# One level of Strassen's scheme for the gate and up projections of a transformer block, in passes of 1024 tokens

## The chip, the cores and the metric

The kernel runs on one core of a Trainium2 chip. The core has five engines that each work through their own list of instructions: TensorE (PE, matrix products, with its weight loads shown apart as PEld), VectorE (DVE), ScalarE (ACT), GpSimd (POOL) and SyncE (SP), which here only issues transfers. Matmul results land in PSUM, eight banks of 512 float32 columns for each of 128 partitions; all else on the chip lives in SBUF. The metric is the device time of one execution in microseconds, given as the median over runs. Beside it stands one execution recorded by the hardware profiler, whose rows are used for all durations.

## What is computed

The reference is one block for 2048 tokens of width 1024: a modulated layer norm, linear attention with 32 heads and a gated residual, a second modulated layer norm, and a gated feed-forward network (FFN) of inner width 3584 with a gated residual.

```python
def _A_ref(x, wqkv, wo):
    ...
    pq, pk = (phi(q), phi(k))
    kv = jnp.einsum('bhsd,bhse->bhde', pk, v)
    z = jnp.einsum('bhsd->bhd', pk)
    num = jnp.einsum('bhqd,bhde->bhqe', pq, kv)
    den = jnp.einsum('bhqd,bhd->bhq', pq, z)[..., None] + 1e-06
    o = num / den
    return (lambda x, *d: x.transpose(*d))(o, 0, 2, 1, 3).reshape(B, S, D) @ wo

def _B_ref(x, w_gate, w_up, w_down):
    return _gelu(x @ w_gate) * (x @ w_up) @ w_down
x = A_x
mod = (_silu(c) @ w_mod).reshape(c.shape[0], 6, 1, -1)
sa, ca, ga, sb, cb, gb = (...)
h = _layernorm(x, axis=-1) * (1 + ca) + sa
x = x + ga * _A_ref(h, A_wqkv, A_wo)
h = _layernorm(x, axis=-1) * (1 + cb) + sb
x = x + gb * _B_ref(h, B_w_gate, B_w_up, B_w_down)
```

Inputs, weights and output are bfloat16 (bf16), sums on the chip float32. Gelu is the tanh form.

## The kernel before

The 2048 tokens are 16 chunks (`c_`) of 128, and four groups (`sg`) of four chunks. The whole of x stays in SBUF (`XALL`) and is overwritten by the block's partial results. One large byte arena holds everything, at offsets worked out by hand, and many tiles share bytes at different times.

The program is written as a list of operations on a small scheduler class, `Sched`. `op` and `dma` record, for each operation, the bytes it reads and writes, and find from these what it must wait for. Each engine then runs its own list. One stretch of the program, from `mark[0]` to `mark[1]`, is handed to `reorder` (L1441), which simulates the engines with a table of costs (`COST`) and puts the lists of DVE, ACT and POOL in order of due time. Everything else, all of TensorE's and SP's lists among it, runs in the order in which it was written. `mark[1]` is set at L1287, ahead of the first normalisation for the FFN.

The stages, with the times in the profiled execution:

- **K, Q** (to 127 us): layer norm 1, the transposed h (`H1`), keys and queries (`L811`, `L862`), and the modulation rows, which DVE adds up from `w_mod` (`mod_step`, L1005, L750).
- **M stage** (127 to 191): `m_tile` (L822, L826) builds keys transposed times x, `kv_prod` (L840, L844) and `w2_pair` (L1118) fold it with the value and output weights into one matrix `W2` of 1024 x 1024, `den` (L1143) makes the denominators, stored and loaded back as row factors (`rb_load`, L1163).
- **Attention outputs** (191 to 234.6 and four more chunks inside the FFN): `pq_scale` (L1176, L1181) scales the queries, `wo_mm` (L1184) multiplies a chunk with `W2`, 16 matmuls a chunk, and adds to x on DVE (L1197). Chunks 0 to 11 run ahead of the FFN; chunks 12 to 15 run as hooks inside the first group's FFN.
- **Layer norm 2**: `ln2_a` (L1272). For chunks 0 to 3 the sums run on ACT and POOL (`ln_stats_act`, L633), for the others on DVE while the group before is in its down projection. A DMA transposes each chunk into `H2`, and `mod2` (L714) scales it on DVE.
- **FFN**, four groups of 512 tokens. `stream_pair` (L1263) loads gate and up weights, 256 columns at a time, into one of three slots; all 7 MB of each are read again for every group. `ffn_fc` (L1318) makes one block of 128 columns: eight matmuls for gate and eight for up into two PSUM banks (L1325, L1328), then Gelu by hand: square and half on ACT, a sum-and-product on DVE, tanh on ACT, two more products on DVE (L1336 to L1343), the result in `YT`. `ffn_down` (L1345) multiplies a chunk with the down weights (56 matmuls), scales with the gate row `GBB` (L1358), adds x (L1360) and stores. The down weights (`WDT`, seven tiles of 1 MB) are loaded once, during the first group.
- The last modulation row, `GBB`, is made during the first group: `gb_load`, `gb_acc`, `gb_rows` (L1382 to L1404).

TensorE's order inside a block, and the rows of Gelu:

```python
for dc in range(NDC):
    og = sch.op(T, lambda e, dc=dc: e.matmul(PS(bg), WG[slot][:, dc, e_ * P:(e_ + 1) * P], H2[sg][:, dc, :], ...
    ou = sch.op(T, lambda e, dc=dc: e.matmul(PS(bu), WU[slot][:, dc, e_ * P:(e_ + 1) * P], H2[sg][:, dc, :], ...
```

Of the kernel before, what the change touches and what calls it, by code (L numbers as in the profile page):

```python
# [6 lines left out]
dt = mybir.dt  # L7
# [3 lines left out]
P = 128  # L11
S = 2048
D = 1024
# [10 lines left out]
NFP = NFC // 2  # L24
HP = 1040
MK = ((684, 341), (0, 342), (342, 342))

GELU_C = math.sqrt(2.0 / math.pi)
GELU_A = 0.044715
# [7 lines left out]
OFF_WD = OFF_HT + NSG * 8192  # L37
OFF_YT = OFF_WD + NFC * 2048
OFF_WS = OFF_YT + NFC * SGW * 2
# [5 lines left out]

OFF_WK = OFF_WD
OFF_WV = OFF_WD + 16384
OFF_WQ = OFF_WD + 32768
OFF_X = OFF_WD + 49152
OFF_MS3 = OFF_YT + 10 * 2048  # L50
OFF_RB = [OFF_WS + 8192, OFF_WD + 16384]
OFF_GAB = OFF_CONST
OFF_GBB = OFF_CONST + 4096
OFF_ROW = OFF_CONST + 8192
OFF_SMALL = OFF_CONST + 12288
OFF_XH2 = OFF_GAB
OFF_PK = [OFF_YT + i * 2048 for i in range(14)] + [OFF_GBB, OFF_GBB + 2048]
OFF_MB = [OFF_TMP + 8192, OFF_TMP + 10240] * 2 + [OFF_WS + i * 2048 for i in range(4)]
OFF_MTB = [OFF_TMP + 6144, OFF_GUH]
OFF_MF = [OFF_TMP + i * 1376 for i in range(2)]  # L60
OFF_MU = [OFF_TMP + i * 1376 for i in range(2, 4)]
OFF_CAR = OFF_HT + 3 * 8192
# [91 lines left out]
class Sched:  # L154
# [41 lines left out]
    def dma(self, stream, fn, rd=(), wr=(), deps=(), note="", overwrite_ok=False):  # L196
# [6 lines left out]
        if prev is not None:  # L203
# [7 lines left out]
              "modr": (0.04, 0.15), "mod": (0.028, 0.15), "w": (0.216, 0.15), "wo": (0.216, 0.15)},  # L211
        ACT_: {"exp": (0.5, 0.1), "sum": (1.19, 0.1), "sq": (1.28, 0.1), "xhata": (1.14, 0.1), "hmoda": (0.49, 0.1), "mcp": (0.38, 0.1), "zc": (0.13, 0.1),
               "mhi": (0.52, 0.1), "mrow": (0.4, 0.1), "wcp": (0.92, 0.1), "hraw": (0.92, 0.1)},
        DVE_: {"min": (0.34, 0.085), "add": (0.607, 0.085), "bn": (0.603, 0.085), "aggr": (0.124, 0.085), "ve": (0.07, 0.085), "xhat": (0.46, 0.085),
               "nm": (0.074, 0.085), "hmod": (0.25, 0.085), "macc": (0.66, 0.085), "mlo": (0.6, 0.085), "kvt": (0.21, 0.085), "z": (0.34, 0.085),
               "dene": (0.335, 0.085), "rden": (1.67, 0.085), "pqs": (0.6, 0.085), "wofold": (1.13, 0.085), "x": (1.14, 0.085)},
        POOL_: {"nmean": (0.22, 0.05), "ve": (0.22, 0.05), "rstd": (0.55, 0.05), "nm": (0.55, 0.05), "ones": (0.12, 0.05)},
        SP_: {"T": (1.25, 1.25), "Tb": (1.25, 1.25), "mT": (1.25, 1.25), "wm": (0.45, 2.9), "wo": (0.45, 2.7), "wv": (0.45, 1.45), "x": (0.45, 2.7), "gab": (0.45, 1.3),
              "sbT": (0.45, 1.3), "cbT": (0.45, 1.3), "rb": (0.45, 1.2), "wg": (0.45, 1.73), "wu": (0.45, 1.73), "rdenst": (0.45, 0.3), "mrowst": (0.45, 0.05)},
# [93 lines left out]
def bass_adaLN_cond__linear_attn_block__geglu_ffn__prompt_kernel(  # L313
# [12 lines left out]
    bf16, f32, i32 = dt.bfloat16, dt.float32, dt.int32  # L326
# [3 lines left out]
    with ExitStack() as es:  # L330
# [16 lines left out]
        H2O = PQO  # L347
        H1 = [at(f"h1T{i}", [P, CPG, NDC, P], bf16, H1O[i]) for i in range(NSG)]
        PQ = [at(f"pq{i}", [P, NG, SGW], bf16, PQO[i]) for i in range(NSG)]
        H2 = [at(f"h2T{i}", [P, NDC, SGW], bf16, H2O[i]) for i in range(NSG)]  # L350
# [4 lines left out]
        WDO = [OFF_WD + fc * 2048 for fc in range(24)] + [HBO[3] + k * 2048 for k in range(4)]  # L355
        WDT = [at(f"wd{q}", [P, 4, D], bf16, WDO[q * 4]) for q in range(7)]
        PK = [at(f"pk{i}", [P, D], bf16, OFF_PK[i]) for i in range(NCH)]
        MB = [at(f"mb{i}", [P, D], bf16, OFF_MB[i]) for i in range(NG)]
        MF = [at(f"mf{i}", [P, 342], f32, OFF_MF[i]) for i in range(2)]
        MU = [at(f"mu{i}", [P, 342], f32, OFF_MU[i]) for i in range(2)]  # L360
        CAR = [at(f"car{i}", [P, D], f32, OFF_CAR + i * 4096) for i in range(2)]
# [7 lines left out]
        YT = at("yT", [P, NFC, SGW], bf16, OFF_YT)  # L369
        WG = [at(f"wg{i}", [P, NDC, 256], bf16, OFF_WS + i * 8192) for i in range(3)]  # L370
        WU = [at(f"wu{i}", [P, NDC, 256], bf16, OFF_WS + i * 8192 + 4096) for i in range(3)]
        GUH = [at(f"guh{i}", [P, SGW], f32, OFF_GUH + i * 2048) for i in range(2)]
# [4 lines left out]
        XHD = [at(f"xhd{i}", [P, D], bf16, OFF_ROW + i * 2048) for i in range(2)]  # L377
        Q1 = [at(f"q1_{i}", [P, SGW], f32, OFF_TMP + i * 2048) for i in range(2)]
        WW = [at(f"ww{i}", [P, SGW], f32, OFF_TMP + 4096 + i * 2048) for i in range(2)]
        TH = [at(f"th{i}", [P, SGW], f32, OFF_TMP + 8192 + i * 2048) for i in range(2)]  # L380
# [4 lines left out]
        WMG = at("wmg", [P, 4, 512], bf16, OFF_GAB)  # L385
        MRG = at("mrg", [P, 512], f32, OFF_GAB)
        HLG = at("hlg", [P, 2, 2, 512], bf16, OFF_ROW)
# [72 lines left out]
        def r_car(i, c0=0, c1=D):  # L460
            return [(OFF_CAR + i * 4096 + c0 * 4, OFF_CAR + i * 4096 + c1 * 4, f"car{i}")]

# [3 lines left out]
        def r_h2(sg, k0=0, k1=NDC, s0=0, s1=SGW):  # L466
            return r_t8(H2O[sg], f"h2T{sg}", k0, k1, s0, s1)

# [6 lines left out]
        def r_wd(fc):  # L475
            return [(WDO[fc], WDO[fc] + 2048, f"wd{fc // 4}")]
# [18 lines left out]
        def r_yt(fc, s0=0, s1=SGW):  # L495
            return [(OFF_YT + (fc * SGW + s0) * 2, OFF_YT + (fc * SGW + s1) * 2, "yT")]

        def r_wg(i):
            return [(OFF_WS + i * 8192, OFF_WS + i * 8192 + 4096, f"wg{i}")]

        def r_wu(i):
            return [(OFF_WS + i * 8192 + 4096, OFF_WS + (i + 1) * 8192, f"wu{i}")]
# [182 lines left out]
        def h2ap(sg, dc, s0, s1):  # L685
            return H2[sg][:, dc, s0:s1]
# [27 lines left out]
        def mod2(c0, n):  # L714
            sg, ci = divmod(c0, CPG)
            mods(h2ap, r_h2, sg, sc2, ci * P, (ci + n) * P, 0, NDC, "h2")
# [24 lines left out]
        MT = (4, 5, 6, 7, 8, 9)  # L741

# [262 lines left out]
        def mod_step():  # L1005
# [3 lines left out]
            if mdone[0] < 48:  # L1009
# [123 lines left out]
        def mod_pass():  # L1133
            assert mdone[0] == 48 and not late
# [49 lines left out]
        def wo_mm(c_, b0, gs):  # L1184
# [9 lines left out]
            if gs[-1] == NG - 1:  # L1194
# [9 lines left out]
                19: "kv4 den1", 20: "w4 rb0.1", 21: "", 22: "kv5", 23: ""}  # L1204
        st = {}

        def hook_run(f):
            if f[:2] == "kv":
                kv_prod(int(f[2:]), 4)
            elif f == "ga":  # L1210
                ga_pass()
            elif f == "modp":
                mod_pass()
            elif f == "z32":
                z32()
            elif f[:3] == "den":
                st[int(f[3:])] = den(int(f[3:]), 5)
                if f == "den0":
# [296 lines left out]
```

## Time and profile before

| what | value |
|---|---|
| median of 3 runs | 833.96 us (833.42 to 834.11) |
| profiled execution, first to last instruction | 831.7 us |
| granted TensorE clock, mean | 1.000 |
| attention outputs, chunks 3 to 11 | 200 to 234.6 us |
| first group, gate and up with four chunks of attention outputs | 234.6 to 345.1 us |
| first group, down | 345.4 to 393.9 us |
| second group, gate and up; down | 393.9 to 490.6; 490.6 to 539.0 us |
| DMA traffic | 121.90 MB, mean 147 GB/s |

The profiled execution is one more run of the same program; the 2.3 us between its span and the median lie around the first and last instruction. A group's row reads: line, engine, operation, what it writes and reads, shape, how often; then busy time in us and the mean of one in ns; then the idle time of the engine just before, and what ended it. The page's other parts that bear on the change are the transfers, in which each row gives the tile, how often, the size and the median time from issue to landing:

```profile
wg<-in_B_w_gate_dram SPq DMA_DIRECT2D x56, 512.0 KB, 4.1
wu<-in_B_w_up_dram SPq DMA_DIRECT2D x56, 512.0 KB, 5.3
rb<-scr_rd SPq DMA_DIRECT2D x32, 256.0 KB, 6.5
wd<-in_B_w_down_dram SPq DMA_DIRECT2D x7, 1024.0 KB, 8.7
```

### The profile page before, as it was taken

How to read it: one execution, taken by the hardware profiler on the slowest of the kernel's cores; microseconds unless marked ns; L12 is line 12 of the kernel's file. 1: busy time of each engine (PE TensorE's matmuls, PEld its weight loads, DVE VectorE, ACT ScalarE, POOL GpSimd, SP SyncE). 2: the span in 40 equal slices, each digit the busy share in tenths (PEclk: the TensorE clock that was granted, in tenths of full speed). 3: DMA queues.
4: the chain of work that ended last, by engine and by line, in shares of the span. 5: the costliest groups of instructions: out<-in, count | busy, mean ns of one | idle time of the engine just before them, and what ended most of it. 6: DMA issues, size and time to landing. Idle time of an engine off the chain costs nothing.

```text
span 831.7 us, 11593 instructions
## 1 busy us (share of the span) xinstructions
PE 826.5 (99%) x4253; PEld 392.3 (47%) x4253; DVE 509.9 (61%) x920; ACT 321.1 (39%) x542; POOL 35.5 (4%) x90
## 2 busy tenths in 40 slices
PE   8999999999999999999999999999999999999998
PEld 4444446665444444444444444444444444444445
DVE  6799888834777577753555565355556535555522
ACT  2597642323523354410444441044444104444300
POOL 2122100000200000000000000000000000000000
DMA  9798769368998788070555533055553306555000
GB/s 286 233 187 220 164 138 262 58 128 196 228 273 240 228 249 256 34 170 19 160 152 152 151 102 76 20 162 154 154 145 102 76 20 170 155 153 137 7 20 26
DMA packets 216929, 121.90 MB, mean 147 GB/s; under 512 B 69276, under 2 KB 206756, under 8 KB 215848
## 3 DMA queue, kind: packets, MB, share of 16 engines
q1 hardware_dynamic: 216856, 121.16, 55.9%
q8 instruction: 34, 0.56, 0.3%
q14 instruction: 23, 0.19, 0.1%
q10 hardware_dynamic: 16, 0.00, 0.0%
HBM read 103.03 MB, written 4.47 MB: 129 GB/s over the span
## 4 chain that ended last, share of the span: by engine, by line
PE 97%; SPq 2%; DMA 1%; issue 0%; DVE 0%
PE ps_all L1353 23%; PE ps_all L1328 23%; PE ps_all L1325 23%; PE ps_all L826 7%; PE ps_all L862 7%; PE ps_all L1189 7%; PE ps_all L811 5%; SPq L568 1%; DMA wmq<-in_w_mod_dram 1%; SPq L573 1%; PE ps_all L844 0%; PE ps_all L1121 0%; PE ps_all L1148 0%; SPq L562 0%; PE ps_all L771 0%
## 5 line engine op out<-in xcount | busy, mean ns | idle before, releaser
L1325 PE MATMUL ps_all<-h2T,wg 128*128 128x512 bf16 x896 | 339.6, 379 | 0.0
L1328 PE MATMUL ps_all<-h2T,wu 128*128 128x512 bf16 x896 | 339.6, 379 | 0.0
L1353 PE MATMUL ps_all<-wd,yT 128*128 128x512 bf16 (+3 forms) x952 | 194.2, 366 | 0.0
L1336 ACT ACTIVATE q<-ps_all 128x512 f32<-128x512 f32 x112 | 66.9, 597 | 224.4 <-PE ps_all L1325 223.2
L1353 PEld LDWEIGHTS ps_all<-wd,yT 128*128 128x128 bf16 x952 | 90.1, 98 | 103.7 <-issue 0.2
L1325 PEld LDWEIGHTS ps_all<-h2T,wg 128*128 128x128 bf16 x896 | 87.7, 98 | 105.7
L1328 PEld LDWEIGHTS ps_all<-h2T,wu 128*128 128x128 bf16 x896 | 87.7, 98 | 105.7
L1341 DVE SCALAR_TENSOR_TENSOR ww<-th,guh 128x512 f32<-128x512 f32 x112 | 77.5, 692 | 77.9 <-ACT th L1340 77.9
L1338 DVE SCALAR_TENSOR_TENSOR ww<-q,ps_all 128x512 f32<-128x512 f32 x112 | 77.0, 687 | 75.8 <-ACT guh L1337 75.7
L1340 ACT ACTIVATE th<-ww 128x512 f32<-128x512 f32 x112 | 70.5, 629 | 86.4 <-DVE ww L1338 86.4
L1358 DVE TENSOR_TENSOR ps_all<-ps_all,gbb 128x512 f32<-128x512 f32 (+3 forms) x34 | 22.7, 667 | 94.6 <-PE ps_all L1353 94.6
L1343 DVE TENSOR_TENSOR yT<-ww,ps_all 128x512 bf16<-128x512 f32 x112 | 76.9, 686 | 3.8
L1337 ACT ACTIVATE guh<-ps_all 128x512 f32<-128x512 f32 x112 | 66.2, 591 | 0.0
L811 PE MATMUL ps_all<-wk,h1T 128*128 128x512 bf16 x248 | 56.8, 379 | 0.4 <-DVE h1T L691 0.2
L862 PE MATMUL ps_all<-h1T,wq 128*128 128x512 bf16 x256 | 56.7, 379 | 0.0
L1189 PE MATMUL ps_all<-w,pq 128*128 128x512 bf16 x256 | 56.6, 379 | 0.0
L800 ACT ACTIVATE eb<-ps_all 128x512 f32<-128x512 f32 x64 | 36.2, 593 | 36.7 <-PE ps_all L811 13.9
L862 PEld LDWEIGHTS ps_all<-h1T,wq 128*128 128x128 bf16 x256 | 25.0, 98 | 29.9
L1189 PEld LDWEIGHTS ps_all<-w,pq 128*128 128x128 bf16 x256 | 24.9, 98 | 30.1 <-ACT w L1123 0.3
L811 PEld LDWEIGHTS ps_all<-wk,h1T 128*128 128x128 bf16 x248 | 23.7, 98 | 28.8 <-DVE h1T L691 2.3
L826 PE MATMUL ps_all<-xall,pk 128*128 128x342 bf16 (+1 forms) x216 | 35.3, 307 | 0.0
L630 ACT ACTIVATE xhd<-xall,nm,rs 128x1024 bf16<-128x1024 bf16 x12 | 14.9, 1240 | 38.2 <-DVE nm L620 31.7
(97 smaller groups left out, 508.3 us busy)
## 6 DMA issues: line engine op xcount, KB each, us to landing
wg<-in_B_w_gate_dram SPq DMA_DIRECT2D x56, 512.0 KB, 4.1
wu<-in_B_w_up_dram SPq DMA_DIRECT2D x56, 512.0 KB, 5.3
rb<-scr_rd SPq DMA_DIRECT2D x32, 256.0 KB, 6.5
wd<-in_B_w_down_dram SPq DMA_DIRECT2D x7, 1024.0 KB, 8.7
wmst<-in_w_mod_dram SPq DMA_DIRECT2D x6, 1024.0 KB, 6.2
wmq<-in_w_mod_dram SPq DMA_DIRECT2D x8, 512.0 KB, 6.7
out_dram<-xall SPq DMA_DIRECT2D x31, 128.0 KB, 1.7
xall<-in_A_x_dram SPq DMA_DIRECT2D x3, 1024.0 KB, 9.5
```

What stands on the lines that cost most here:

```text
L811: o = sch.op(T, lambda e, dc=dc: e.matmul(PS(bank), H1[sg][:, ci, dc, :], W_[:, dc, jg * 512:(jg + 1) * 512], start=(dc == 0), stop=(dc == ...
L826: o = sch.op(T, lambda e, c_=c_: e.matmul(PS(bank, 0, n), PK[c_][:, g * P:(g + 1) * P], xrow(c_, o_, o_ + n), start=(c_ == 0), stop=(c_ == ...
L862: o = sch.op(T, lambda e, dc=dc: e.matmul(PS(b), WQ[:, dc, qc * P:(qc + 1) * P], H1[sg][:, :, dc, :], start=(dc == 0), stop=(dc == NDC - 1 ...
L1189: last[half] = sch.op(T, lambda e, g=g, half=half: e.matmul(PS(b0 + half), PQ[sg][:, g, ci * P:(ci + 1) * P], W2[:, g, half * 512:(half + ...
L1325: og = sch.op(T, lambda e, dc=dc: e.matmul(PS(bg), WG[slot][:, dc, e_ * P:(e_ + 1) * P], H2[sg][:, dc, :], start=(dc == 0), stop=(dc == ND ...
L1328: ou = sch.op(T, lambda e, dc=dc: e.matmul(PS(bu), WU[slot][:, dc, e_ * P:(e_ + 1) * P], H2[sg][:, dc, :], start=(dc == 0), stop=(dc == ND ...
L1336: sch.op(A, lambda e: e.activation(Q1[j][:, :], PS(bg), ACTF.Square, scale=math.sqrt(GELU_A)), prd=pr(bg), wr=rq, note=f"q1 {fc}")
L1338: sch.op(V, lambda e: e.scalar_tensor_tensor(WW[j][:, :], Q1[j][:, :], 1.0, PS(bg), op0=ALU.add, op1=ALU.mult), rd=rq, prd=pr(bg), wr=rw, ...
L1340: sch.op(A, lambda e: e.activation(TH[j][:, :], WW[j][:, :], ACTF.Tanh, scale=GELU_C), rd=rw, wr=rt, note=f"th {fc}")
L1341: sch.op(V, lambda e: e.scalar_tensor_tensor(WW[j][:, :], TH[j][:, :], 1.0, GUH[j][:, :], op0=ALU.add, op1=ALU.mult), rd=rt + rg, wr=rw, n ...
L1343: sch.op(V, lambda e: e.tensor_tensor(YT[:, fc, :], WW[j][:, :], PS(bu), ALU.mult), rd=rw, prd=pr(bu), wr=r_yt(fc), note=f"yT {fc}")
L1353: o = sch.op(T, lambda e, b=b, fc=fc, c0=c0, c1=c1, n=n: e.matmul(PS(b, 0, n), YT[:, fc, ci * P:(ci + 1) * P], WDT[fc // 4][:, fc % 4, c0:c1],
```

## The change

Gate and up are computed with one level of Strassen's scheme (Winograd's form). A pass takes 1024 tokens, as two halves of 512 (`H2[0]`, `H2[1]`); the 1024 inputs are two halves of four blocks; a unit takes 256 columns of gate and of up, as two halves of 128. Instead of eight half-size products a unit makes seven for each of gate and up (`t`), of four matmuls each. Products 1 and 2 read the bf16 data; products 3 to 7 read sums of halves of the tokens (`SS`, four tiles made once in a pass, and `A22R`, a copy) and of the weights (`TP`, five tiles, made in every unit), all in float32r, four bytes an element. Results are put together in PSUM: ACT copies the first product to a second bank (`pcp`), later products accumulate there, and DVE adds the saved fifth product (`escp`, `padd`).

Gelu is one ACT instruction (`Gelu_apprx_tanh`) and one DVE product. There are two passes of 14 units, each followed by the down projection of eight chunks; the down weights lie in other tiles' bytes and are loaded in each pass. All 16 chunks of attention outputs run before the first unit, layer norm 2 of chunks 0 to 7 runs on ACT and POOL beside them, and a second `reorder` covers this stretch and the first two units. The row `GBB` is made in the M stage. The core of the diff:

```diff
-        H2O = PQO
+        H2O = [HBO[3], OFF_GAB]
+        H2 = [at(f"h2{'ab'[i]}", [P, NDC, SGW], bf16, H2O[i]) for i in range(2)]
+        A22R = at("ar", [P, NDC // 2, SGW], f32r, HBO[0])
+        SS = [at(f"ss{i}", [P, NDC // 2, SGW], f32r, OFF_SS[i]) for i in range(4)]
+        TP = [at(f"tp{i}", [P, 2, NDC // 2, P], f32r, OFF_TP[i]) for i in range(5)]
+        WT = [at(f"wt{i}", [P, 2, NDC, 256], bf16, OFF_WS + i * 8192) for i in range(2)]
...
+        def s_sums(p, pool):
+            def two(eng, i, k, in0, in1, op, rd):
+                sch.op(eng, lambda e: e.tensor_tensor(SS[i][:, k:k + 2, :], in0, in1, op), rd=rd, wr=r_ss(i, k, k + 2), note=f"ssum{i} {p}.{k}")
+            a, b = H2
+            for k in (0, 2):
+                two(G if 0 in pool else V, 0, k, b[:, k:k + 2, :], b[:, ND2 + k:ND2 + k + 2, :], ALU.add, r_h2(1, k, k + 2) + r_h2(1, ND2 + k, ND2 + k + 2))
...
+        def t_sum(u, k):
+            if k == 3:
+                ap, rd = wq(u, 1, 1)
+                for t in range(2):
+                    sch.op(A, lambda e, t=t: e.activation(TP[3][:, t, :, :], ap[:, t, :, :], ACTF.Copy), rd=rd[t:t + 1], wr=r_tp(3, t, t + 1), note=f"brcp u{u}")
+                return
...
+            for t in range(2):
+                sch.op(V, lambda e, t=t: e.tensor_tensor(TP[k][:, t, :, :], in0[:, t, :, :], in1[:, t, :, :], ALU.subtract),
...
+        def prod(u, t, k):
...
+            b = {1: BA, 2: BA, 5: BE, 6: BB, 7: BB, 4: BB, 3: BC}[k] + t
+            fresh = k in (1, 5)
+            for dc in range(ND2):
+                (l_, rl), (r_, rr) = lhs(dc), rhs(dc)
+                o = sch.op(T, lambda e, l_=l_, r_=r_, dc=dc: e.matmul(PS(b), l_, r_, start=fresh and dc == 0, stop=dc == ND2 - 1, skip_group_check=True),
...
+        def unit(p, u):
+            more = u + 1 < NFP
+            for t in range(2):
+                prod(u, t, 1)
+                if held[0]:
+                    held[0]()
+                    held[0] = None
+                pcp(t)
+            t_sum(u, 4)
+            for t in range(2):
+                prod(u, t, 5)
+                escp(t)
+            if more:
+                t_sum(u + 1, 0)
+            for t in range(2):
+                prod(u, t, 6)
+                padd(t, BC)
+            prod(u, 0, 2)
+            ia = gi[0] % 2
+            gelu(BA)
+            prod(u, 1, 2)
+            if u + 2 < NFP:
+                wt_dma(u + 2)
+            y_out(ia, BA, f1, 0)
+            if more:
+                t_sum(u + 1, 1)
+            for t in range(2):
+                prod(u, t, 7)
+                padd(t, BE)
+            gelu(BE)
+            y_out(ie, BE, f2, 1)
+            prod(u, 0, 3)
+            gelu(BC)
+            prod(u, 1, 3)
+            y_out(ic, BC, f2, 0)
+            if more:
+                t_sum(u + 1, 3)
+                t_sum(u + 1, 2)
+            prod(u, 0, 4)
+            gelu(BB)
+            prod(u, 1, 4)
+            held[0] = lambda: y_out(ib, BB, f1, 1)
...
-        for c_ in range(3, 12):
+        for c_ in range(3, NCH):
...
+            if 3 <= c_ < 10:
+                ln2(c_ - 2, True)
+            if c_ == 8:
+                wt_dma(1)
+            if c_ == 7:
+                mod2_act(0)
+            if c_ == 8:
+                mod2(1, 0, 2)
+            if c_ == 10:
+                mod2(1, 2, 2)
+        s_sums(0, (0, 2))
+        ar_copy(0)
+        for k in range(4):
+            t_sum(0, k)
+        for p in range(2):
+            c0 = p * 2 * CPG
+            for u in range(NFP):
+                unit(p, u)
+                if p == 0 and u == 1:
+                    mark.append(sch.n)
+                if p == 0 and u in (2, 4):
+                    wd_dma(u // 2 - 1)
+                if u == NFP - 2:
+                    wd_dma(2)
...
+            for q in (5, 3, 6, 4):
+                wd_dma(q)
+            ga_, gb_ = range(c0, c0 + CPG), range(c0 + CPG, c0 + 2 * CPG)
+            for c_ in (c0, c0 + 3, c0 + 1, c0 + 2):
+                down_q(c_, (0,), first=True)
+            for q in (1, 2, 3, 5):
+                for c_ in ga_:
+                    down_q(c_, (q,))
+            if p == 0:
+                for c_ in range(2 * CPG, NCH):
+                    ln2(c_, False)
...
         sch.reorder(mark[0], mark[1], (DVE_, ACT_, POOL_), {id(x4_op): 8.0})
+        sch.reorder(mark[1], mark[2], (DVE_, ACT_, POOL_), {})
```

`wd_dma(q)` loads one tile of 1 MB of down weights; `wt_dma(u)` loads the 256 gate and 256 up columns of unit `u` into one of two slots; `down_q` runs four column blocks of down for one chunk into two PSUM banks, so that the weights are used tile by tile over four chunks.

## The prediction

> **What bounds the kernel now.** I read the engine totals and the chain of waits first, then the costliest groups, a table by stage, and the timeline of the stage where the change starts.
>
> ```profile
> PE 826.5 (99%) x4253; PEld 392.3 (47%) x4253; DVE 509.9 (61%) x920; ACT 321.1 (39%) x542; POOL 35.5 (4%) x90
> ...
> PE 97%; SPq 2%; DMA 1%; issue 0%; DVE 0%
> ...
> L1325 PE MATMUL ps_all<-h2T,wg 128*128 128x512 bf16 x896 | 339.6, 379 | 0.0
> L1328 PE MATMUL ps_all<-h2T,wu 128*128 128x512 bf16 x896 | 339.6, 379 | 0.0
> ...
> L1325 PEld LDWEIGHTS ps_all<-h2T,wg 128*128 128x128 bf16 x896 | 87.7, 98 | 105.7
> ```
>
> TensorE is never idle for long (99%, 97% of the chain), so time falls only if its stream gets shorter and nothing new holds it up. A matmul's 379 ns is latency, not spacing; spacing comes from the chain in order of time and from the stage table (columns: stretch and its length; busy time of PE, its weight loads, DVE, ACT, POOL; granted clock; DMA share; GB/s).
>
> ```profile
> 200.08 34.53 PE ps_all L1189 x160
> ...
> 345.45 48.45 PE ps_all L1353 x224
> ```
> ```profile
> 394.00:490.60 96.60, 96.60 (x449) 43.78 (x448) 56.78 (x83) 46.40 (x82) 0.00 (x0) 1.00 0.53 143
> ```
>
> 48.45 us over 224 matmuls is 0.216 us each, and the second token group's gate and up take 96.6 us over 448: again 0.216, at full clock. Each weight load of 98 ns lies under the matmul before it.
>
> **What is removed.** Before, gate and up are 4 groups x 28 column blocks x 16 = 1792 matmuls: 387.1 us. After, 2 passes x 14 units x 7 products x 2 (gate, up) x 4 = 1568 matmuls of the same shape: 338.7. Difference 224 x 0.216 = **-48.4 us**, if each still costs 0.216. The down projection keeps 896 full-width matmuls' worth of work, the attention outputs keep 16 x 16; both only move.
>
> **The float32r price.** Only products 1 and 2 stay bf16; 28 units x 5 x 2 x 4 = 1120 matmuls read float32r on both sides. No row shows one. Low end: as bf16, nothing added. High end from the nearest rows: the load of the weights, 98 ns, no longer lies under the previous matmul, 1120 x 0.098 = +110 us. The bf16 load fills 98 of 216 ns, so even a load twice as long still fits (196 ns) as long as it runs ahead of its matmul. I take 0: same array shape, one column per step, and hidden. Break-even is 42/1120 = 37 ns per matmul (the forecast below lies 42 under the median).
>
> The Trainium skill speaks against this in two places. "FP8 and Floating Point Precision", section "TensorE Precision Notes", has true FP32 as four passes through the array but a reduced form that truncates to 22 bits; were float32r the former, an estimate by that page is 1120 x 3 x 0.216 = 726 us more. "TensorE: Matmul & The Clock Gate", section "Weight-path perf modes", gives the fast weight load only to inputs that are not FP32; its slower load, columns divided by 1.2, is 107 ns here, still under 216, so the sum stays, or loses 120 us if exposed. No run here shows either yet.
>
> **DVE and ACT inside a unit.** One unit is 56 x 0.216 = 12.1 us of TensorE. DVE has eight 128x512 weight sums, four PSUM sums and four products. The nearest rows, for every mix of types and memories:
>
> ```profile
> L1341 DVE SCALAR_TENSOR_TENSOR ww<-th,guh 128x512 f32<-128x512 f32 x112 | 77.5, 692 | 77.9 <-ACT th L1340 77.9
> ...
> L1343 DVE TENSOR_TENSOR yT<-ww,ps_all 128x512 bf16<-128x512 f32 x112 | 76.9, 686 | 3.8
> ...
> L1337 ACT ACTIVATE guh<-ps_all 128x512 f32<-128x512 f32 x112 | 66.2, 591 | 0.0
> ```
>
> 16 x 0.69 = 11.0 of 12.1 us; the scales at L1181 run four in 2.48 us, 0.62 apart, which would make it 9.9. ACT: two copies PSUM to PSUM, two to SBUF, two weight copies, four Gelu, 10 x 0.59 = 5.9. Both fit, DVE with little to spare. The tightest hand-off is product 4, whose bank the second PSUM sum must have read: product 2 ends 6.9 us into the unit; then 0.25 of hop, one product, two weight sums and the sum itself, 4 x 0.69, give 9.9 against 10.4 where product 4 starts. Slack 0.5. Low end nothing; high end 0.3 a unit (8 us). I take 1 us in all. The first Gelu loads a table on ACT: the only such load in the trace takes 1.28 us, so 0 to 1.3; I take 1, since unit 0 is when DVE is fullest. The old chain square-ww-tanh-ww (3 DVE and 3 ACT per block) goes; it was hidden, and is worth nothing. Weight traffic for gate and up halves (1 MB per 12.1 us, was 1 MB per 6.9); down weights come twice, 7 MB more. The first pass's last loads wait for the last unit's buffers and land within about 9 us each (the page's 8.7 for such a load), while queue order gives them 20 to 35 us of down work first: 0.
>
> **The start of the FFN.** All of chunks 12 to 15's outputs (64 matmuls, 13.8 us) move ahead, so gate would start where 234.6 is now plus 13.8 = 248.4. But it now needs normalised tokens of eight chunks, not four, plus operand sums. One chunk's normalisation on ACT now:
>
> ```profile
> 203.10 1.06 ACT L638 ACTIVATE xh<-xall 128x1024 bf16<-128x1024 bf16 x1 [1.96 <-DMA rb<-scr_rd]
> 204.07 0.19 ACT L638 ACTIVATION_READ_ACCUMULATOR xh<-xall 128x1 f32 x1
> 204.67 1.15 ACT L641 ACTIVATE xh<-xall,mv 128x1024 bf16<-128x1024 bf16 x1 [0.42 <-POOL mv L639]
> 205.73 0.19 ACT L641 ACTIVATION_READ_ACCUMULATOR xh<-xall,mv 128x1 f32 x1
> 207.86 1.24 ACT L630 ACTIVATE xh<-xall,nm,rs 128x1024 bf16<-128x1024 bf16 x1 [1.95 <-POOL nm L646]
> 209.01 1.04 ACT L638 ACTIVATE xh<-xall 128x1024 bf16<-128x1024 bf16 x1
> ```
>
> It repeats every 5.5 to 6.0 us with 3.8 busy. The order is the program's now (the planner's range ends ahead of it); the change adds a second planned range over this stage, so chunks can interleave. Eight chunks from 203.1: 234 at 3.8 each, 249 at 5.8. Then the transpose, by the view of the tile it writes in this stage:
>
> ```profile
> DMA to landing us min/median/max: 3.2/8.3/10.3
> ```
>
> That is 8.3 us median (DMA is full there, share 1.02 in 191 to 235). After it come the last modulations, 8 at 0.27 = 2.1 us, then on POOL the first operand sum. Its nearest row, from the groups by form:
>
> ```profile
> L549 POOL TENSOR_SCALAR ident<-iota_a 128x128 bf16<-128x128 int32 x1 | 0.6, 569 | 0.1
> ```
>
> No POOL row has 1024 elements: low end DVE's 1.22 us (the residual add L1197), high end the slope of L549 against a 128x1 form (0.57 less 0.19 over 127 elements), 3 ns each, 3.3 us. Two halves: 2.4 to 6.6. Product 5 wants it at 250.1. Early end: 234 + 8.3 + 2.1 + 2.4 = 246.8, no wait. Late end: 249 + 8.3 + 2.1 + 6.6 = 266, less 250.1 = 16, and product 7's sum, also on POOL behind the first, adds perhaps 2. So 0 to 18. DVE is loaded too: 13 residual adds and three left over (16 x 1.22), 24 scales (15), modulation (4.3), its operand sums (4.9) and weight sums (4.1) make 48 us in the 50 from 200 to 250. I take **+4**, nearer the early end, since ACT alone would be done at 234. While product 5 waits, every later matmul stands behind it on TensorE, and the copies on ACT and sums on DVE that follow them are late by the same; nothing else is on the path. Nothing is gained here: there was no idle time to recover.
>
> SP's queue: the transposes now share the stage with chunk 12 to 15's row factors (2 MB), the last 1 MB of x, the gate row (0.5 MB) and 2 MB of gate and up weights, in program order, while the old stage's next loads (down, w_mod) have gone elsewhere; that is in the 8.3.
>
> **The last modulation row** moves from the first FFN group to the M stage (127 to 191 us), where DVE is busy 43 of 64 us: 16 x 0.74 + 2 x 0.69 = 13 us more fits. Its four loads of 512 KB go into a DMA-full stretch (share 0.94 in 127 to 150) ahead of the transposes feeding L844: one load is 2 us at 247 GB/s. 0 to 2; I take 0.5.
>
> **Between the passes** normalisation and sums of eight chunks (DVE: 2.6 us a chunk, 16 modulations, six sums of 1.22, together 33) lie under 48 us of down work, and the evacuations (2.8 us a chunk) under 3.45: 0; without that cover the start's 4 would return. The tail is unchanged.
>
> **Sum.** 831.7 - 48.4 + 4 + 1 + 1 + 0.5 = 789.8 of span; the median of the runs lies 2.3 above the profiled span: **792 us**. Own range: 785 (no wait anywhere) to 806 (14 more at the start).
>
> **Rivals.**
> 1. *Waits eat part of it.* The start at its late end (+14) and 0.3 per unit (+8): 814, spread 806 to 832. For: DVE's 48 of 50 us and the slack of 0.5. Against: the planner orders the start by due times.
> 2. *Exposed float32r weight loads; slower.* Place: every product but 1 and 2. Price 98 ns x 1120: 792 + 110 = 902; it decides from 37 ns on. For: no row shows a float32r load ahead of its matmul. Against: 118 ns of room beside each bf16 load.
> 3. *DVE becomes the bound.* If a weight sum with float32r output cost 1.22 us (a 1024-wide row), a unit needs 8 x 1.22 + 8 x 0.69 = 15.3: 28 x 3.2 = 90, 882; slower from 1.0 us a sum. Against: every 128x512 row is 0.68 to 0.75.
> 4. *The change doesn't do what it says*: one float32r matmul is several array passes. Two would cost 1120 x 0.216 = 242: 1034.
>
> **How the numbers follow.** Forecast 0.64; rival 1, 0.12; a price just at break-even 0.02; rival 2, 0.15; 3, 0.04; 4, 0.03. A measurement of this kernel tells about 0.2% (1.7 us) from no change. Faster: 0.64 + 0.12 = 0.76; same 0.02; slower 0.22. The range runs from 785 through rival 1 and break-even to 840, where the cheapest part of rival 2 adds about 0.02: 0.80.
>
> **What would show it.** Right: float32r matmuls 0.216 apart, a unit of 12.1 us, TensorE at 97% or more, two gate-and-up stretches near 169 us, a wait of a few us near 250. Wrong: spacing above 0.25 in products 3 to 7 but not in 1 and 2 (rival 2), TensorE waiting on DVE's weight sums every unit (3), or a hole of ten us or more before product 5 (1).

## The result and the profile after

| | before | after |
|---|---|---|
| median | 834.03 us (833.42 to 834.11) | 820.32 us (819.34 to 821.04) |
| profiled execution, first to last instruction | 831.7 us | 819.2 us |

Each median is over four runs; the 833.96 us given with the profile before came from three of them. The changed kernel takes 0.9835 of the time, 95% interval 0.9821 to 0.9849: a gain of 13.7 us where 42 were predicted. The direction was right, and the time lies inside the wide range of 785 to 840 but outside the forecast's own, 785 to 806: two thirds of the gain are missing. The page of the changed kernel, engine totals, shares of the chain, and the groups that answer to those shown before:

```profile
PE 794.4 (97%) x3962; PEld 468.4 (57%) x4029; DVE 571.1 (70%) x990; ACT 311.2 (38%) x523; POOL 55.1 (7%) x108
...
PE 39%; DVE 2%; issue 1%; DMA 1%; ACT 1%; SPq 0%; POOL 0%; DVEq 0%; POOLq 0%
...
L1404 PE MATMUL ps_all<-ss,tp 128*128 128x512 f32 x896 | 227.5, 406 | 8.3 <-DVE h2b L694 5.5
L1486 PE MATMUL ps_all<-wd,yT 128*128 128x512 bf16 (+3 forms) x934 | 196.0, 370 | 6.9 <-DVE xall L1479 6.0
L1404 PEld LDWEIGHTS ps_all<-ss,tp 128*128 128x128 f32 x896 | 170.1, 190 | 50.5 <-DVE h2b L694 6.0
...
L1379 DVE TENSOR_TENSOR tp<-wt 128x512 fp32r<-128x512 bf16 x112 | 74.6, 689 | 44.8 <-PE ps_all L1486 25.3
...
L1404 PEld LDWEIGHTS ps_all<-h2a,wt 128*128 128x128 bf16 x448 | 39.5, 98 | 54.2 <-issue 14.1
```

Three things are new against the page of before. TensorE waits where it waited for nothing: 8.3 us ahead of the products of sums (L1404) and 6.9 ahead of the down matmuls (L1486). A float32r weight load takes 190 ns, the bf16 one beside it 98. And the chain's shares add up to some 45%, where they covered nearly all before: followed back from the end, the chain is lost at 455 us, so its 39% for PE says nothing of the first half. The waits come out one by one in the view of what each engine waited for (total us, times, longest):

```profile
PE ps_all L1486 <- DVE xall L1479: 6.0, 1, 6.0
PE ps_all L1404 <- DVE h2b L694: 5.5, 1, 5.5
PE ps_all L1404 <- POOL ss L1350: 2.4, 1, 2.4
```

Each occurs once: two at the start of the FFN, one between the passes. None repeats per unit. That leaves a loss that no wait shows, and the chain in order of time has it. The first row starts 12.60 us ahead of the second, unit by unit, through the whole second pass:

```profile
561.48 12.53 PE ps_all L1404 x55
574.08 12.53 PE ps_all L1404 x55
```

A unit was to take 56 x 0.216 = 12.1. The matmuls' starts within it, in the trace, are 216 ns apart for bf16 and 227 for float32r (now and then 231 to 236).

The stages can be summed as the prediction summed them:

| stage | if it ran as predicted without waits | measured | lost |
|---|---|---|---|
| gate and up start at | 248.4 | 248.97 | 0.6 |
| 28 units | 28 x 12.09 | 28 x 12.60 | 14.3 |
| first gate and up, beyond 14 x 12.60 | 0 | 188.47 - 176.4 | 12.1 |
| first down stretch, beyond 96.8 | 0 | 105.81 - 96.8 | 9.0 |
| second gate and up, beyond 14 x 12.60 | 0 | 176.41 - 176.4 | 0 |

-48.4 + 0.6 + 14.3 + 12.1 + 9.0 = -12.4; the spans differ by -12.5. The last three rows go by the first matmul of each stretch in the trace. The 12.1 and the 9.0 are more than the waits of 8.3 and 6.0 in them. The table by stage (stretch and length; busy time and count of PE, weight loads, DVE, ACT, POOL; granted clock; DMA share; GB/s) has the rest:

```profile
255.00:260.00 5.00, 1.19 (x2) 0.50 (x2) 4.89 (x5) 1.18 (x2) 4.32 (x3) 0.56 0.00 0
260.00:265.00 5.00, 4.61 (x10) 3.21 (x11) 4.72 (x3) 2.48 (x3) 3.03 (x1) 0.50 0.00 0
265.00:270.00 5.00, 4.93 (x20) 3.30 (x21) 3.83 (x5) 0.60 (x1) 0.00 (x0) 0.92 0.21 56
...
488.00:492.00 4.00, 0.04 (x1) 0.05 (x2) 3.97 (x6) 0.00 (x0) 0.00 (x0) 0.89 0.00 0
492.00:496.00 4.00, 4.00 (x10) 1.44 (x11) 3.90 (x7) 0.00 (x0) 0.00 (x0) 0.50 0.29 98
496.00:500.00 4.00, 4.00 (x15) 1.60 (x14) 3.90 (x7) 0.00 (x0) 0.00 (x0) 0.76 0.29 98
...
543.20:719.60 176.40, 175.44 (x771) 124.89 (x783) 139.72 (x219) 77.42 (x138) 0.00 (x0) 1.00 0.32 90
```

The last row is the second gate-and-up stretch, at full clock. After each wait TensorE's granted clock is 0.50: 10 matmuls fall in the 4 us from 492, where 18 fit. In the trace it stays at half for 10.2 us at the start (255.6 to 265.8, the second wait among them) and for 6.8 between the passes (491.1 to 497.9), and matmuls there start 427 ns apart. That accounts for 9.0 - 6.0 = 3.0 us between the passes and for 2.8 of the 12.1 - 8.3 = 3.8 us at the start; the other 1.0 lies around the waits themselves, which count only from the end of the matmul before, 379 ns after its start, or 628 at half clock. The Trainium skill, "TensorE: Matmul & The Clock Gate", section "Part 1: The HAM clock gate (the "warmup" mystery)", says that the clock falls to half after an idle window of about 3.4 us and needs about as long a busy one to come back. The fall agrees (waits of 5.5 and 6.0 us); the way back took 6.0 us of matmuls between the passes, longer than that. And the length of a wait decides nothing by itself here: one of 2.2 us in the last experiment below was followed by half clock, one of 2.9 us in the first was not.

What the start waits for is in the timeline (start, length, engine, line, operation, idle before):

```profile
244.87 2.13 DVE L694 TENSOR_SCALAR h2b<-h2b,cb1T,sbT 128x256 bf16<-128x256 bf16 x8
...
251.10 5.76 DVE L694 TENSOR_SCALAR h2b<-h2b,cb1T,sbT 128x256 bf16<-128x256 bf16 x8 [0.70 <-DMA h2b<-xl]
251.83 2.12 POOL L1350 TENSOR_TENSOR ss<-h2a,h2b 128x1024 fp32r<-128x1024 bf16 x1 [7.89 <-ACT ps_all L1409]
254.11 2.15 POOL L1350 TENSOR_TENSOR ss<-h2b 128x1024 fp32r<-128x1024 bf16 x1 [0.16 <-DVE h2b L694]
256.78 1.21 DVE L1350 TENSOR_TENSOR ss<-ss,h2a 128x1024 fp32r<-128x1024 f32 x1
256.94 3.03 POOL L1350 TENSOR_TENSOR ss<-h2b 128x1024 fp32r<-128x1024 bf16 x1 [0.68 <-DVE h2b L694]
258.10 2.95 DVE L1350 TENSOR_TENSOR ss<-h2a,ss 128x1024 fp32r<-128x1024 bf16 x1
```

Two causes stand here. First, the tokens come late: the last eight modulations start at 251.1, when DVE's wait for their transpose ends. Secondly, the same eight modulations take 5.76 us beside POOL's sums, and 2.13 at 244.87, where POOL is idle. Two of the eight take 2.16 and 2.14 us, the others 0.33 to 0.35; those two start 0.04 and 0.10 us after a POOL sum and end 0.08 us after it. A DVE sum beside POOL takes 2.95 us instead of 1.21. That is no slower rate: one engine stands still while the other's instruction runs. The Trainium skill, "SBUF — State Buffer", section "SBUF: two separate sides", has it: VectorE's second pair of ports is shared with GpSimd under an exclusive lock, held for a whole instruction. The prediction priced POOL's sums beside DVE's work, with nothing for one holding up the other.

Why the tokens come late is in ACT's list:

```profile
216.10 0.19 ACT L644 ACTIVATION_READ_ACCUMULATOR xl<-xall,mv 128x1 f32 x1
222.56 1.06 ACT L641 ACTIVATE xl<-xall 128x1024 bf16<-128x1024 bf16 x1 [6.27 <-DMA h2a<-xl]
...
240.75 0.80 ACT L723 ACTIVATE h2a<-h2a,sbT,cb1T 128x512 bf16<-128x512 bf16 x1
...
242.59 2.21 ACT L723 ACTIVATE h2a<-h2a,sbT,cb1T 128x512 bf16<-128x512 bf16 x3
244.71 1.23 ACT L633 ACTIVATE xl<-xall,nm,rs 128x1024 bf16<-128x1024 bf16 x1
```

The normalised chunks lie in a ring of four tiles (`XL`), and a tile is free when its transpose has read it. ACT stands 6.27 us for that, until the first transpose has landed. SP's list, with the times in which it issues:

```profile
211.82 3.85 SPq L673 DMA_TRANSPOSE h2a<-xl  x1
215.72 1.94 SPq L1318 DMA_DIRECT2D wt<-in_B_w_gate_dram  x1
217.71 3.60 SPq L1318 DMA_DIRECT2D wt<-in_B_w_up_dram  x1
221.40 2.63 SPq L673 DMA_TRANSPOSE h2a<-xl  x1
```

The view of `h2a`, whose transposes these are, has the times from issue to landing:

```profile
DMA to landing us min/median/max: 5.5/7.2/10.7
```

The first transpose is the longest, issued at 211.82 and landed at 222.47; the last loads of row factors and x that SP had issued before it landed from 217.8 to 220.1, and the gate row's load (L827) stands between. The weight loads of the first unit come behind it, so ACT's wait is not theirs. They stand ahead of the second transpose, whose chunk was normalised at 215.2 and which is issued at 221.40.

The last normalisation ends at 245.9, not at the 234 that ACT's busy time allowed. The 6.27 us are the largest single piece of this; another is work that the 3.8 us a chunk leave out: ACT also modulates the first half's tokens (L723), and four of these eight, 3.0 us, stand in its list ahead of the last normalisation. Between the passes the same kind of thing shows on DVE:

```profile
464.80 2.14 DVE L694 TENSOR_SCALAR h2b<-h2b,cb1T,sbT 128x256 bf16<-128x256 bf16 x8 [10.81 <-DMA h2b<-xl]
...
477.97 5.79 DVE L694 TENSOR_SCALAR h2b<-h2b,cb1T,sbT 128x256 bf16<-128x256 bf16 x8 [5.86 <-DMA h2b<-xl]
483.67 2.35 DVE L1350 TENSOR_TENSOR ss<-h2b 128x1024 fp32r<-128x1024 bf16 x2
...
490.49 0.69 DVE L1478 TENSOR_TENSOR ps_all<-ps_all,gbb 128x512 f32<-128x512 f32 x1
```

This stretch runs in the order written. DVE stands 10.81 us for the transposes of chunks 12 and 13 ahead of the statistics of chunks 14 and 15, then 5.86 for theirs, then slows beside POOL, and has three pairs of sums, all before the first evacuation (L1478), for which TensorE's banks wait until 491.96.

### The profile page after: what moved, and what is told of

Same layout as the page of the kernel before. It is cut to its first block, busy times and chain, and to the rows that moved or that the text cites. A ratio compares the mean times of both kernels' runs of the same rounds, so it can differ in the third digit from the quotient of the medians.

```text
span 819.2 us, 10821 instructions
## 1 busy us (share of the span) xinstructions
PE 794.4 (97%) x3962; PEld 468.4 (57%) x4029; DVE 571.1 (70%) x990; ACT 311.2 (38%) x523; POOL 55.1 (7%) x108
## 5 line engine op out<-in xcount | busy, mean ns | idle before, releaser
L1404 PE MATMUL ps_all<-ss,tp 128*128 128x512 f32 x896 | 227.5, 406 | 8.3 <-DVE h2b L694 5.5
L1486 PE MATMUL ps_all<-wd,yT 128*128 128x512 bf16 (+3 forms) x934 | 196.0, 370 | 6.9 <-DVE xall L1479 6.0
L1404 PEld LDWEIGHTS ps_all<-ss,tp 128*128 128x128 f32 x896 | 170.1, 190 | 50.5 <-DVE h2b L694 6.0
L1486 PEld LDWEIGHTS ps_all<-wd,yT 128*128 128x128 bf16 x952 | 90.7, 99 | 112.2 <-DVE xall L1479 6.5
L1420 ACT ACTIVATE ge<-ps_all 128x512 f32<-128x512 f32 x112 | 64.3, 596 | 137.6 <-DVE ps_all L1415 74.7
L1379 DVE TENSOR_TENSOR tp<-wt 128x512 fp32r<-128x512 bf16 x112 | 74.6, 689 | 44.8 <-PE ps_all L1486 25.3
L1404 PE MATMUL ps_all<-h2a,wt 128*128 128x512 bf16 x420 | 100.1, 380 | 1.9
L1424 DVE TENSOR_TENSOR yT<-ge,ps_all 128x512 bf16<-128x512 f32 x112 | 74.7, 685 | 33.3 <-PE ps_all L1404 30.6
L1415 DVE TENSOR_TENSOR ps_all<-ps_all,es 128x512 f32<-128x512 f32 x112 | 75.7, 697 | 20.3 <-PE ps_all L1404 20.3
L1478 DVE TENSOR_TENSOR ps_all<-ps_all,gbb 128x512 f32<-128x512 f32 (+3 forms) x34 | 22.6, 666 | 76.2 <-PE ps_all L1486 76.2
L1379 DVE TENSOR_TENSOR tp<-wt,tp 128x512 fp32r<-128x512 bf16 x112 | 72.2, 686 | 0.0
L1404 PEld LDWEIGHTS ps_all<-h2a,wt 128*128 128x128 bf16 x448 | 39.5, 98 | 54.2 <-issue 14.1
L1404 PE MATMUL ps_all<-ar,tp 128*128 128x512 f32 x224 | 55.3, 389 | 0.0
L1404 PEld LDWEIGHTS ps_all<-ar,tp 128*128 128x128 f32 x224 | 42.0, 188 | 8.7
```

The source lines that it names most:

```text
L1379: sch.op(V, lambda e, t=t: e.tensor_tensor(TP[k][:, t, :, :], in0[:, t, :, :], in1[:, t, :, :], ALU.subtract), rd=r0[t:t + 1] + (r1[t:t + ...
L1404: o = sch.op(T, lambda e, l_=l_, r_=r_, dc=dc: e.matmul(PS(b), l_, r_, start=fresh and dc == 0, stop=dc == ND2 - 1, skip_group_check=True) ...
L1415: sch.op(V, lambda e: e.tensor_tensor(PS(dst + t), PS(BB + t), ES[t][:, :], ALU.add), prd=pr(BB + t), rd=r_2k(OFF_ES[t], f"es{t}"), pwr=pr ...
L1420: sch.op(A, lambda e: e.activation(GE[i][:, :], PS(b), ACTF.Gelu_apprx_tanh), prd=pr(b), wr=r_2k(OFF_GE[i], f"ge{i}"), note="gelu")
L1424: sch.op(V, lambda e: e.tensor_tensor(YT[:, fc, h * SGW:(h + 1) * SGW], GE[i][:, :], PS(b + 1), ALU.mult), rd=r_2k(OFF_GE[i], f"ge{i}"), p ...
L1486: o = sch.op(T, lambda e, fc=fc: e.matmul(PS(b, 0, n), YT[:, fc, ci * P:(ci + 1) * P], WDT[fc // 4][:, fc % 4, c0:c1], start=first and fc ...
```

## The experiments

Theory at the outset: the 28 us of missing gain are the float32r rate, an order between the passes that puts evacuations behind transposes, and a start that is late through SP's queue and POOL beside DVE. Rivals stand with each run. Nine kernels were run. Each had the kernel before run on the same chip, at 833.8 to 834.4 us.

### 1. The sums in bf16

```diff
-        A22R = at("ar", [P, NDC // 2, SGW], f32r, HBO[0])
+        A22R = at("ar", [P, NDC // 2, SGW], bf16, HBO[0])
...
-        TP = [at(f"tp{i}", [P, 2, NDC // 2, P], f32r, OFF_TP[i]) for i in range(5)]
+        TP = [at(f"tp{i}", [P, 2, NDC // 2, P], bf16, OFF_TP[i]) for i in range(5)]
```

`SS` likewise; the sums are rounded to bf16.

> The sums of token halves and weight halves (and the two copies) are kept in bf16, not float32r; everything else as changed. The sums are rounded more coarsely, so the output differs in its last bits. Theory (float32r matmuls cost 227 ns where bf16 ones cost 216): products 3 to 7 fall to 0.216 apart, a unit goes from 12.60 to 12.10 us, two passes of 14 units give back 28 x 0.50 = 14 us: about 806. Rival (the 0.5 us of a unit is lost in hand-offs between TensorE and DVE or ACT, or in the change of data type between products): a unit stays above 12.4 us and the time above 814.

Measured: 799.5 us (798.69 to 800.93), ratio 0.9591 (0.9575 to 0.9607), 20.8 below the changed kernel and 6.5 below the 806 expected. The second gate-and-up stretch takes 169.21 us, 14 x 12.09: every matmul 0.216 apart, and float32r's whole price is 28 x 0.51 = 14.3 us. The other 6.5 lie in the two places where TensorE waits, and DVE's sums got lighter too:

```profile
L1404 PEld LDWEIGHTS ps_all<-ss,tp 128*128 128x128 bf16 x896 | 87.8, 98 | 115.4 <-DVE h2b L694 6.1 <-POOL ss L1350 3.0 <-issue 1.6
L1379 DVE TENSOR_TENSOR tp<-wt 128x512 bf16<-128x512 bf16 x112 | 44.8, 422 | 62.1 <-PE ps_all L1404 38.1 <-PE ps_all L1486 23.4 <-DMA wt<-in_B_w_gate_dram 0.4
```

A weight sum takes 422 ns, not 689. The first down stretch takes 99.8 us, 6.0 less, for the wait in it falls from 6.0 to 2.9 us and the clock stays full behind it; the start's waits stay, 5.7 and 2.1. The stretch with the wait of 2.9 us:

```profile
440.00:500.00 60.00, 57.11 (x265) 25.75 (x264) 28.94 (x58) 11.51 (x13) 6.44 (x6) 1.00 0.30 73
```

### 2. What makes a float32r matmul 11 ns longer

In the first pass each product uses 64 of 128 weight columns (the other half of each block's gate and up results is left out); in the second, each matmul is cut into two of 256 columns.

```diff
+ parts = ((ps_all[0:64, b * 512:(b + 1) * 512], l_[:, 0:64], r_),)   # first pass
+ parts = tuple((PS(b, c0, c0 + 256), l_, r_[:, c0:c0 + 256]) for c0 in (0, 256))   # second
```

> Measures what sets 227 ns. In pass 0 every gate and up matmul loads 64 of its 128 weight columns (the other half of its results is left out); in pass 1 it loads all 128 and streams its 512 tokens as two matmuls of 256, each with its own weight load. Theory (the float32r weight load, 188 ns against 98 in bf16, sets the pace): pass 0's float32r matmuls are 216 apart with loads near 110 ns, a unit 12.1 us; pass 1's stay near 227 apart although they stream half as much, a unit 40 x 2 x 0.227 + 16 x 0.216 = 21.6 us. Rival (reading four bytes an element slows the stream itself by 5%): pass 0 stays at 227, 12.6 us a unit; pass 1's fall to about 114, 12.6 us a unit or a little more.

Measured: one time of 833.98 us, and neither theory. The second pass, by stage:

```profile
560.00:700.00 140.00, 140.00 (x1200) 135.37 (x1199) 110.14 (x172) 61.42 (x109) 0.00 (x0) 1.00 0.29 78
```

1200 half matmuls in 140 us are 0.117 each; the starts are 120 ns apart for float32r and 109 for bf16, and (80 x 120 + 32 x 109) / 112 gives that mean. In the first pass float32r is 230 ns apart (median) though its weight load fell from 190 to 136 ns. (At each change between bf16 and float32r the starts are 309 to 327 ns apart there, four changes a unit, so the whole stretch takes 195.0 us, more than before; what sets this stays open.) So between matmuls of one type the load's length does not set the pace, and neither does a share of the stream, which would halve with the columns: the difference is 11 ns at 512 and 11 at 256. It is a fixed amount per matmul. What it is spent on stays open.

### 3. The order between the passes

```diff
                     ln2(c_, False)
-                    if c_ == 3 * CPG - 1:
-                        mod2_act(0)
-                    if c_ in (NCH - 3, NCH - 1):
-                        mod2(1, c_ % CPG - 1, 2)
-                s_sums(1, (2,))
+                mod2_act(0)
+                mod2(1, 0, 2)
+                mod2(1, 2, 2)
             for c_ in ga_:
                 down_q(c_, (6, 4), last=True)
+            if p == 0:
+                s_sums(1, (2,))
```

> Only the order in which the work between the passes is written changes: all eight normalisations first, then the modulations, then the evacuation of the first four down chunks, then the operand sums. Theory (TensorE's 6.0 us wait at 486 is the evacuation standing on DVE's list behind sums that wait for transposes, and the half clock after it costs 3 us more): no wait in the down stretch of pass 0, 96.8 us in place of 105.8, so 820 - 9 = 811. Rival (DVE or the transposes are simply too slow for the work, whatever the order): the wait moves to the first unit of pass 1, 6 us or more, time 818 or above.

Measured: 811.87 us (811.53 to 812.27), ratio 0.9733 (0.9719 to 0.9748): 8.5 below the changed kernel. The chain in order of time through that stretch:

```profile
437.30 96.71 PE ps_all L1486 x448
```

448 x 0.216 = 96.8, so nothing is lost, clock included. The order alone made the 9.0 us, as expected (811).

### 4. The operand sums all on DVE

```diff
-        s_sums(0, (0, 2))
+        s_sums(0, ())
...
-                s_sums(1, (2,))
+                s_sums(1, ())
```

> The first and third operand sums, six of which the changed kernel gives to POOL, go to DVE. Theory (a sum on POOL slows DVE beside it: the last eight modulations take 5.76 us at 251 and 5.79 at 478 against 2.13 for the eight before them): modulations back to 2.1 us, product 5 starts about 3 us earlier in pass 0 and the pass boundary is 1 to 3 us shorter; against that DVE gets 1.2 us for each half sum. Net -2 to -5 us, 815 to 818. Rival (the modulations are slow for another reason, and DVE, full at the start, is the bound): no gain or 2 to 4 us slower, 820 to 824.

Measured: 815.39 us (814.61 to 816.78), ratio 0.9777 (0.9763 to 0.9792), 4.9 below and inside the expected 815 to 818. The first gate-and-up stretch takes 183.12 us, 5.3 less, and the first down stretch 104.28, 1.5 less. DVE does four more sums at the start and two more between the passes, and is done sooner:

```profile
251.17 2.14 DVE L694 TENSOR_SCALAR h2b<-h2b,cb1T,sbT 128x256 bf16<-128x256 bf16 x8 [0.34 <-DMA h2b<-xl]
253.22 2.35 DVE L1350 TENSOR_TENSOR ss<-h2b 128x1024 fp32r<-128x1024 bf16 x2
```

The modulations are back at 2.14 us, and the clock at the start is at half for 3.4 us instead of 10.2. POOL's help cost more than it gave.

### 5. The loads that stand ahead of the transposes

The gate row's load moves behind unit 3, unit 0's weights from the first chunk to the fifth of the loop (`c_ == 7`), unit 1's one chunk later.

```diff
-        wt_dma(0)
...
-            if c_ == 8:
+            if c_ == 7:
+                wt_dma(0)
+            if c_ == 9:
                 wt_dma(1)
```

> Only SP's order changes: the gate row (0.5 MB) is loaded in unit 3, not ahead of the attention outputs, and unit 0's weights (1 MB) after the sixth transpose, not after the first; unit 1's one chunk later. Theory (the start is late because the normalised chunks' transposes stand behind bulk loads: ACT idled 6.3 us at 216 for a buffer that a transpose had not yet read): ACT's idle time there shrinks by 4 us or more, the last normalisation ends 4 to 6 us earlier than 245.9, pass 0's gate-and-up stretch falls from 188.5 to 179 to 184 us, time 811 to 816. Rival (DVE's 48 us of work in the stage, or POOL beside it, is the bound): stretch above 186, time 818 or more.

Measured: 821.19 us (820.43 to 821.74), ratio 0.9847 (0.983 to 0.9863): no gain, where 811 to 816 was expected. The last chunk is normalised 2.0 us earlier and ACT's idle time shrinks to 4.75 us only: of the 6.27 us the moved loads had made 1.5. DVE gives all of it back:

```profile
248.82 5.76 DVE L694 TENSOR_SCALAR h2b<-h2b,cb1T,sbT 128x256 bf16<-128x256 bf16 x8
...
257.26 2.61 DVE L1377 TENSOR_TENSOR tp<-wt,tp 128x512 fp32r<-128x512 bf16 x1
```

The modulations start 2.3 us sooner and still run beside POOL, and the first unit's weight sums, whose data now come later, fall into the same stretch and are blocked too (2.61 us for 0.69).

### 6. The three together

Edits 3, 4 and 5, in float32r.

> The new order between the passes, SP's new order and all operand sums on DVE, together, float32r kept. Theory (three separate losses): start and boundary both close, pass 0's stretch 177 to 179 us (14 x 12.60 = 176.4 and a little), the first down stretch 96.8: 820 - 9 - 10 = 799 to 803. Rival (the start is bound by DVE, which now has the sums too): stretch stays above 182 and the time above 805.

Measured: 806.13 us (805.7 to 807.96), ratio 0.9671 (0.9656 to 0.9685), above the expected 799 to 803. The first gate-and-up stretch still loses 182.09 - 176.39 = 5.7 us and starts 1.8 us later, all of which came about ahead of the attention outputs (their first matmul starts at 193.7 instead of 191.9), where the kernels do not differ. DVE works nearly without a pause from 244 on, and TensorE waits for it in small pieces, the largest of them in this row:

```profile
PE ps_all L1402 <- DVE ss L1348: 2.1, 4, 1.1
```

### 7. The three together, sums in bf16

> As the run before, with the sums in bf16 as in the first experiment (rounded more coarsely). Theory (the terms add up: 48.4 for the matmuls left out, nothing given back but the start's rest): a unit of 12.10 us, stretches of 169 to 172 and 169.3, down 96.8: 834 - 48 + 1 to 3 = 787 to 789. Rival (the losses overlap, one hides another): 791 or above.

Measured: 787.41 us (786.64 to 787.8), ratio 0.9441 (0.9427 to 0.9455), as expected. The first gate-and-up stretch takes 169.92 us, the second 169.21, down 96.7, and the whole execution runs at a granted clock of 1.000:

```profile
PE 773.8 (99%) x3959; PEld 369.4 (47%) x4029; DVE 503.5 (64%) x996; ACT 314.9 (40%) x523; POOL 38.9 (5%) x102
```

It beats both kernels, 46.4 us under the one before on the same chip, with the operand sums rounded to bf16. Of those that keep float32r, run 6 is the fastest measured, with run 8 below no different from it.

### 8 and 9. Without the moved loads

Edits 3 and 4 alone, in float32r and in bf16.

> The float32r kernel with the order of the pass boundary and with the operand sums on DVE, and the loads where the change has them. If the later weight loads of the three-part kernel (806.13 us) cost at the start what they saved in the queue, this one gains what the two parts gained alone, 820.3 - 8.5 - 5.3 = 806.5, within 1.5 of the three-part kernel, with gate starting near 249.0 instead of 250.8 and the first gate-and-up stretch near 183. If the later loads were worth something beside the other two parts, it is at 808 or more.

> The same two parts with the operand sums rounded to bfloat16 (half their bytes). All matmuls 0.216 us apart; first gate-and-up stretch 169 to 173, first down stretch 96.7, second gate-and-up stretch 169.2. If the later loads were worth nothing: within 1.5 us of 787.4, the three-part kernel with the same rounding, gate starting 1.8 earlier. If they were worth something beside lighter sums on DVE: 789 or more.

Measured: 807.04 us (806.1 to 807.95), ratio 0.9671 (0.9655 to 0.9687), and 792.43 us (792.18 to 793.4), ratio 0.9499 (0.9485 to 0.9513). In float32r the two parts add up (8.5 + 4.9 = 13.4 by runs 3 and 4, 13.3 off 820.3 measured), and the moved loads are worth nothing measurable (807.0 against 806.1). With sums in bf16 run 9 takes 792.4 - 787.4 = 5.0 us more than run 7. Of this 4.1 lies in the first gate-and-up stretch (174.05 against 169.92), where the moved loads act; the profiled executions also differ by 1.5 us ahead of the attention outputs, where the kernels are the same. The two pairs fit this reading, which no run tests by itself: float32r sums fill DVE, so tokens that come sooner wait there; with light sums DVE has room, and the tokens' arrival decides. In run 9 the last modulations start at 252.00, 1.3 us behind gate's first matmul, and in run 7 at 248.04, 1.1 ahead of it. Run 9's one long wait, and what the clock does after it:

```profile
254.79 5.49 PE L1404 MATMUL ps_all<-ss,tp 128*128 128x512 bf16 x16 [2.24 <-DVE ss L1350]
```
```profile
254.00:256.00 2.00, 1.21 (x5) 0.42 (x6) 2.00 (x5) 1.23 (x2) 0.00 (x0) 1.00 0.00 0
256.00:258.00 2.00, 2.00 (x7) 0.69 (x5) 1.75 (x3) 1.00 (x2) 0.00 (x0) 0.53 0.00 0
258.00:260.00 2.00, 2.00 (x7) 0.78 (x6) 0.70 (x1) 0.19 (x1) 0.00 (x0) 0.62 0.00 0
```

The matmuls are 216 ns apart just after the wait; then, for 3.4 us, 427. Run 6's waits, none over 1.1 us, left the clock at 1.00.

## Why the prediction was right and wrong

The span came out at 819.2 us against 789.8. The float32r rate makes 14.3 of the 29.4, the stretch between the passes 9.0 and the start 12.1 instead of 4; the two terms of 1 us for the inside of a unit and for the Gelu table cost next to nothing. So the steps that failed are two terms set to 0, the float32r price and the work between the passes, and one that was mis-sized, the start.

- **What is removed, -48.4: right.** Without float32r a unit takes 12.09 us (runs 1 and 7), 1568 matmuls at 0.216.
- **The float32r price, taken as 0 with bounds 0 and +110: mis-sized.** It is 11 to 13 ns a matmul, 14.3 us in all. The argument that a load twice as long still hides held: it takes 190 ns of 227 and runs ahead (the 107 ns worked out from the page were too few). What failed is the sentence that same array shape and one column per step mean the same spacing. The break-even of 37 ns a matmul was the right yardstick, and the rivals of exposed loads (+98 ns) and of several passes (+216) are refuted.
- **DVE and ACT inside a unit, +1, and DVE as a rival bound: right in kind.** DVE's weight sums take 0.69 us, and in the second pass DVE is busy 139.7 of 176.4 us, 10.0 of 12.6 in a unit. TensorE waits in no unit but the first, so the hand-offs cost nothing.
- **The start of the FFN, +4 from bounds 0 to 18: mis-sized, and chosen at the wrong end.** It cost 12.1, inside the bounds. The early end counted ACT's 3.8 us of busy time a chunk; ACT's list also holds modulations, and it stood 6.27 us for the first transpose to free a tile. The prediction counted a transpose's landing once, at the end ("that is in the 8.3"). The medians were no longer than that, 7.2 and 5.0 us for the two halves, but the first took 10.7, and with four tiles in the ring it held ACT up as well; the wait before a transpose is issued, 6.2 us for the second, is not in a landing time either. Moving the loads ahead of the transposes alone gained nothing (run 5). Two more things were left out: POOL's sums do not run beside DVE's work (run 4: 5.3 us), and after the waits the clock is at half, which costs 2.8 us of the 12.1. With edits 3 to 5 and light sums the stretch loses 0.7 (run 7).
- **Between the passes, taken as 0: failed by the order of the work.** It set 33 us of DVE work against 48 us of down matmuls and called it hidden. Busy time fits; the order does not, for DVE works through its list in order and stands 16.7 us for transposes inside it. The prediction named what would happen "without that cover", at the price of the start, 4; it was 9.0 (run 3).
- **The last modulation row, +0.5: nothing speaks against it.** Gate starts at 248.97, with the row in the M stage, against 248.4. It cannot be told more closely: in the runs, whose kernels do not differ ahead of the attention outputs, gate starts anywhere from 248.97 to 250.8.
- **The Gelu table, +1:** in run 7 the first stretch is 0.7 us longer than the second in all, so less than 1.

The first rival, waits at the start at its late end and 0.3 us a unit, gave 814 and came nearest. Its start, 18 us at the late end, was 6 too much; its amount per unit is there, 0.51 for 0.3, but it is matmul rate and not a wait; and it has nothing for the 9.0 between the passes. That its sum comes near is in part luck.

## What to carry to other kernels

Work that is hidden by its busy time is hidden only if its place in each engine's list is right: for every moved piece, follow the list of each in-order engine past every transpose it will wait for, and look at what stands behind. Before giving a piece of VectorE's work to GpSimd, count the time as added to VectorE's own, wherever VectorE has work that uses the same ports. And a repeated instruction in a new number format deserves a bound per instruction, since some 12 ns on each of 1120 matmuls were a third of the expected gain.

## What the runs showed of the hardware

- A float32r matmul starts 227 ns after the one before it instead of 216 with 512 columns, 120 instead of 109 with 256: a fixed 11 ns. It is a single pass. The Trainium skill, "FP8 and Floating Point Precision", section "TensorE Precision Notes", gives four passes for true FP32; nothing like it was seen here. Its weight load takes 188 to 190 ns, bf16's 98. With 64 weight columns the two take 134 to 136 and 109 (run 2).
- VectorE beside GpSimd: a 128x256 modulation takes 2.16 us instead of 0.34, a 128x1024 sum 2.95 instead of 1.21, and the other way round a GpSimd sum 3.03 to 3.11 instead of 2.12.
- A single wait of 2.2 us was followed by 3.4 us at half clock (run 9), and those of 5.5 and 6.0 us in the changed kernel by 10.2 and 6.8 us: such a wait of TensorE costs more than its length. One of 2.9 us left the clock full (run 1), as did four of at most 1.1 us (run 6), so no threshold can be read from these runs.
- VectorE's sum of two bf16 tiles takes 422 ns into bf16 and 689 into float32r, for 128x512.
